# An mLSTM and mixture-of-experts attention kernel on one core: a rebuilt front, expert ranks on GpSimd and ScalarE, a shorter PSUM hold, and values loaded without zeros

## Chip, cores and metric

The kernel runs on one core of one Trainium2 chip. The metric is device time in microseconds of one execution. Before the change the median of three runs is 352.0 us (350.49 to 353.44).

## The reference

For 4 sequences of 768 tokens and 8 heads of 40, an mLSTM recurrence with exponential gates and a running maximum produces x (768 x 320 for each sequence). Four experts then run causal attention over x, and each token takes the weighted sum of its two best experts.

```python
m_new = np.maximum(f_gate[:, :, t] + m, i_gate[:, :, t])
f_stab = np.exp(f_gate[:, :, t] + m - m_new)
i_stab = np.exp(i_gate[:, :, t] - m_new)
C = f_stab * C + i_stab * outer(v_t, k_t)
n = f_stab * n + i_stab * k_t
y_t = sigmoid(o_gate_t) * (C @ q_t) / np.maximum(np.abs(n @ q_t), 1.0)
...
logits = x @ w_gate
topk = np.argpartition(-logits, K, axis=-1)[..., :K]
w = softmax over the two logits that were taken
for e in range(E):
    q, k, v = x @ wq[e], x @ wk[e], x @ wv[e]
    a = causal softmax of scale * (q @ k.T)
    out += (w of the tokens that took e) * (a @ v @ wo[e])
```

## The kernel before

**How it is written.** Nothing is issued directly. `Tape.add` records every operation, and `Tape.plan` (L339 on) simulates the five engines and the DMA queue with a cost for each operation (`cost`), and writes down the order in which it placed them. `emit` (L541) then issues them in that order, so L541 is the line of nearly every instruction. Within an engine the order is fixed. Between engines semaphores hold. A change of one operation or of one cost therefore re-orders the whole program.

**Part 1** is the mLSTM in 24 chunks of 128 tokens (4 sequences, 6 chunks each), each cut into two sub-chunks of 64. `gates` works out the running maximum m, the gates' sums G and the input factor for 32 rows (sequence and head) in three segments of tokens: 0 to 127, 128 to 383, 384 to 767. `gates_out` transposes the input factor and writes it to `cN`; `decays` makes the factors `dec` of the carried state. `p1_prep` makes the decay matrix `dm` and the weighted keys `ks`; `p1_intra` makes scores within the chunk; `p1_inc` steps the state (`cd`, `sts`); `p1_scale` multiplies the queries `kqs` by exp(G); `p1_state` adds the part within the chunk (matmuls of `nat` and `dm`) and the carried part (matmuls of `kqs` and `sts`) in one PSUM bank, divides, and multiplies by the output gate into `xt`; `p1_out` transposes to `xh` and `xl`, a high and a low half.

For the first three chunks (the front) `dm` and the factor on `kqs` come from TensorE matmuls that spread G over the partitions. For all others they come from DRAM: G and exp(G) are written to `gd` and `ge` and read back, spread over partitions, as `dm` and `eqs`.

**Part 2** is the attention in 8 units (a sequence's half, 384 tokens). Its head is three `values`, two `queries`, two `keys` and `gate`, which makes the logits' ranks `rk` and the weights `ew`. Then come scores (`big` banks), softmax (`A`), transposes (`AT`), `mix` (with the shares `facb`, made from `ew`) and `project` to `ob` and the output. Units overlap with later chunks of part 1; the two are interleaved by hand in `flow`.

**Buffers and queues.** PSUM has four banks `one` and two pairs `big`. Nearly all DMAs go through SyncE's queue, in order. Each chunk brings 2 for `kqs`, 2 for `qbd`, 2 for `dm`, 2 for `eqs` and 1 for `nat`. The `nat` tile holds a chunk's keys (320 columns), its values in 656 columns, of which half are zeros (so that a sub-chunk's matmul sees its own 64 tokens only), and its output gate (320).

**Dummies.** 16 matmuls of zeros (`wz`) open the program. 60 more are spares: `choose` puts one where the next group of matmuls is more than 200 ns away, before it looks for another group that could start.

Of the kernel before, what the change touches and what calls it, by code (L numbers as in the profile page):

```python
# [33 lines left out]
    ("nat", 3, NNAT),  # L34
# [30 lines left out]
C_IDENT, C_CAUS, C_HALF, C_INDB = 0, 128, 192, 194  # L65
C_SEL = C_INDB + 4
C_MASK = C_SEL + 4 * GR
NKV = DM + 2 * H * D1


def const_table():
# [13 lines left out]
    t[64:, C_HALF] = 1.0  # L85
    t[:, C_HALF + 1] = 1.0
    t[64:, C_HALF + 1] = -1.0
# [73 lines left out]
class Tape:  # L161
# [95 lines left out]

    def cut(self):
        self.open = None


    def cost(self, op):
        n = max([x.free_size() for x in op.ins + op.outs[:1]] or [1])
        psum = any("PSUM" in str(x.space) for x in op.ins)
        if op.call == "dma_start":
# [16 lines left out]
            return 600.0, total / d * (10 + d * 0.05) / k, k, 1600.0  # L282
        if op.eng == "tensor":
            return (0.0, 0.0)
        if op.call == "memset":
            return (n / 1.2 + 60, 40) if op.eng == "gpsimd" else (n * 0.52 + 8, 75)
        if op.eng == "gpsimd":
            inner = any([s for s, c in x.ap if c > 1][-1:] == [0] for x in op.ins)
            return (120 + n * (1.85 if inner else 2.32), 40) if op.call != "tensor_copy" else (130 + n * 2.0, 40)
        if op.eng == "scalar":  # L290
            return n / 1.2 + (53 if psum else 93) + (95 if len(op.outs) > 1 else 0), 120
        if op.call == "tensor_tensor_scan":
            return n * 2.1 + 120, 92
        if op.call == "tensor_tensor_reduce":
            return n * 1.0417 + 230, 92
# [12 lines left out]
    def plan(self):  # L308
# [47 lines left out]
        free = dict.fromkeys(ENGINES, 700.0)  # L356
        colfree, mode, order = [700.0] * 4, None, []
        rings = [0.0] * 16
        pool = [0.0, 0.0]
# [54 lines left out]
        def choose():  # L414
# [7 lines left out]
            if spares:  # L422
                b = self.home(spares[0])
                if b.ring.holder[b.slot or 0] is b:
                    x = begin(spares[:1])
                    if x is not None and (s is None or s - x > STALL):
                        return x, 0, spares[:1]
# [19 lines left out]
            if best:  # L447
                return best
            return (s, 0, todo[0]) if s is not None else None

        while len(order) < len(ops) + spare:
            best = None
            for e in ENGINES:
                if e == "tensor":
                    c = choose()
                else:
                    cand = []
                    for op in avail[e]:
# [4 lines left out]
                        if op.call == "dma_start":  # L463
                            s = max(s, op.late + shift - HOLD)
# [48 lines left out]
            if op.call == "dma_start":  # L513
# [5 lines left out]
                op.end = en + 700  # L519
            else:  # L520
                if e == "vector" and pool[0] < s < pool[1] and blocked(op):
                    s = pool[1]
                free[e] = s + op.cost[0]
# [35 lines left out]
def mlstm_moe_kernel(ctx, tc, kq, nat, ig, fg, wqkv, wo, const, out):  # L559
# [63 lines left out]
    eqs = [keep(f"eqs{i}", [GR, 4, P], F32) for i in range(2)]  # L623
    sts = [keep(f"sts{i}", [GR, 4, 2, D1], F32) for i in range(6)]
    qls = [keep(f"qls{i}", [P, 2, HALF], F32R) for i in range(3)]
    gd = dram("gd", [B * H, S])
    ge = dram("ge", [B * H, S])
    cN = keep("cN", [P, NCH, 2, B, 4], F32)
    gend = gtail.rearrange("p (b j) -> p b j", b=B)
# [33 lines left out]
    def load_nat(b, j, t=None, part=None):  # L663
        if t is None:
            t = buf("nat", [P, NNAT], F32)
        cs = slice(0, NNAT) if part is None else (slice(0, NKV), slice(NKV, NNAT))[part]
        (nc.sync.dma_start(t[:, cs], nat[b, j][:, cs]))
        return t

# [23 lines left out]
    def gates(c0, c1, eng):  # L693
# [5 lines left out]
        nc.gpsimd.tensor_tensor(i_sb[:, cs], i_sb[:, cs], m_sb[:, cs], op=ALU.subtract)  # L699
        yield  # L700
        eng.tensor_tensor(f_sb[:, n0:c1], f_sb[:, n0:c1], m_sb[:, n0 - 1 : c1 - 1], op=ALU.add)
        eng.tensor_tensor(g_sb[:, n0:c1], f_sb[:, n0:c1], m_sb[:, n0:c1], op=ALU.subtract)
        eng.tensor_scalar(g_sb[:, cs], g_sb[:, cs], -104.0, None, op0=ALU.max)
        yield
        nc.vector.tensor_tensor_scan(G_sb[:, cs], rmask[:, cs], g_sb[:, cs], 0.0, op0=ALU.mult, op1=ALU.add)
        gdone.append(nc.gpsimd.tensor_tensor(i_sb[:, cs], i_sb[:, cs], G_sb[:, cs], op=ALU.subtract))
# [912 lines left out]
```

## Time and profile before

| | us |
|---|---|
| median of 3 runs (lowest, highest) | 352.0 (350.49, 353.44) |
| profiled execution, its own time | 352.23 |
| its span, first to last instruction | 350.5 |
| PE / PEld busy | 324.0 (92%) / 275.1 (79%) |
| DVE busy | 265.8 (76%) |
| ACT busy | 217.7 (62%) |
| POOL busy | 188.7 (54%) |

PE is TensorE's matmuls, PEld its weight loads, DVE is VectorE, ACT is ScalarE, POOL is GpSimd, and SPq is SyncE's queue, which issues DMAs. Busy PE counts each matmul's latency, not its share of the array, so 92% is not 92% of peak. Tiles are named without their numbers. A group's row gives its count, total busy us, mean ns, and the idle time ahead of it.

### The profile page before, as it was taken

Reading aid. Unit: us, or ns where it says so; the run is one execution under the profiler, and the core shown is the slowest. Engines: PE = TensorE matmul, PEld = TensorE weight load, DVE = VectorE, ACT = ScalarE, POOL = GpSimd, SP = SyncE. Lnnn points to the kernel's source line nnn. Section 1 sums busy time; section 2 is a strip of 40 time slices with the busy share of each in tenths; the row PEclk is TensorE's granted clock in tenths of the full one; section 3 lists DMA queues with packets and bytes.
Section 4 is the critical chain, followed back from the end, with each engine's and each line's share of the span. In section 5 each row is a group of like instructions: output and inputs, shape, how many; then the busy total and the mean of one; then the engine's idle time right before and its main releaser. Section 6 shows DMA issues by size and latency. Waiting matters only on the chain.

```text
span 350.5 us, 9216 instructions
## 1 busy us (share of the span) xinstructions
PE 324.0 (92%) x3312; PEld 275.1 (79%) x3312; DVE 265.8 (76%) x787; ACT 217.7 (62%) x591; POOL 188.7 (54%) x267
## 2 busy tenths in 40 slices
PE   8789998899998998899999998799999999999994
PEld 3576696798887887588998787679998887988882
DVE  7999389879888867669888767569888766677673
ACT  5673245776785776544785666534785776567752
POOL 4783698689758456648538456638547221241000
PEclk9999999999999999999999999999999999999999
DMA  7999929957375266427585257427570100101001
GB/s 200 288 240 230 214 76 242 240 146 199 117 194 140 49 186 191 109 80 186 163 196 154 38 143 220 112 51 212 173 197 6 56 0 2 39 20 38 21 21 37
DMA packets 40653, 45.78 MB, mean 131 GB/s; under 512 B 3808, under 2 KB 34752, under 8 KB 40608
## 3 DMA queue, kind: packets, MB, share of 16 engines
q1 hardware_dynamic: 40560, 45.10, 49.1%
q8 instruction: 26, 0.43, 0.5%
q14 instruction: 19, 0.16, 0.2%
q10 hardware_dynamic: 48, 0.10, 0.1%
HBM read 41.06 MB, written 4.13 MB: 129 GB/s over the span
## 4 chain that ended last, share of the span: by engine, by line
PE 56%; DVE 23%; issue 6%; ACT 6%; DMA 5%; POOL 2%; SPq 1%; DVEq 0%; POOLq 0%; ACTq 0%
PE one L541 48%; PE big L541 8%; DVE AT L541 4%; DVE sts L541 3%; DMA dm<-gd 2%; DVE KS L541 2%; DVE one L541 2%; DVE A L541 2%; DMA eqs<-ge 2%; ACT A L541 2%; ACT AT L541 2%; DVE rk L541 2%; DVE den L541 1%; DVE xt L541 1%; ACT KS L541 1%
## 5 line engine op out<-in xcount | busy, mean ns | idle before, releaser
L541 ACT ACTIVATE A<-A,nmx 128x128 f32<-128x128 f32 (+5 forms) x96 | 63.7, 666 | 18.1 <-DVE nmx L541 17.7
L541 DVE CUSTOM_DVE_ANT_0 A<-big,maskw 128x128 f32<-128x128 f32 (+5 forms) x96 | 58.1, 618 | 6.1 <-PE big L541 4.5
L541 PE MATMUL one<-cst,A 128*128 128x128 f32 x336 | 53.1, 277 | 8.4 <-ACT AT L541 3.1
L541 PEld LDWEIGHTS one<-cst,A 128*128 128x128 f32 x336 | 39.5, 140 | 16.6 <-ACT AT L541 4.6
L541 ACT ACTIVATE AT<-one 128x512 f32<-128x512 f32 (+2 forms) x101 | 41.0, 427 | 17.4 <-PE one L541 11.2
L541 PE MATMUL big<-KS,QD 128*128 128x384 f32 (+4 forms) x128 | 44.6, 357 | 1.0 <-DVE nmx L541 0.8
L541 PE MATMUL one<-AT,V 128*64 128x384 f32 (+2 forms) x360 | 40.1, 368 | 0.4 <-DVE R L541 0.4
L541 PE MATMUL big<-KS,qls 128*128 128x384 f32 (+4 forms) x128 | 40.2, 322 | 0.0
L541 POOL TENSOR_TENSOR cd<-sts,dec 112x328 f32<-112x328 f32 x37 | 27.4, 742 | 20.2 <-DVE sts L541 19.6
L541 POOL TENSOR_TENSOR dm<-dm,cst 128x512 f32<-128x512 f32 x21 | 27.0, 1287 | 20.0 <-DMA dm<-gd 14.2
L541 PEld LDWEIGHTS one<-AT,V 128*64 128x64 f32 x360 | 22.8, 137 | 15.8 <-issue 12.3
L541 PE MATMUL one<-xh,WH 128*128 128x384 f32 x96 | 34.4, 358 | 0.2
L541 PE MATMUL one<-xl,WH 128*128 128x384 f32 x96 | 32.4, 337 | 0.0
L541 POOL TENSOR_TENSOR kqs<-kqs,eqs 112x512 f32<-112x512 f32 x21 | 26.9, 1283 | 6.5 <-DMA eqs<-ge 6.2
L541 DVE TENSOR_TENSOR sts<-one,cd 40x164 f32<-40x164 f32 x80 | 25.7, 321 | 5.0 <-POOL cd L541 3.0
L541 PEld LDWEIGHTS big<-KS,QD 128*128 128x128 f32 x128 | 24.4, 191 | 2.3 <-DVE nmx L541 1.4
L541 DVE SCALAR_TENSOR_TENSOR qls<-one,QD 64x384 fp32r<-64x384 f32 x32 | 17.7, 554 | 11.2 <-ACT QD L541 7.1
L541 PE MATMUL one<-qbd,kqs 112*64 112x128 f32 x384 | 26.2, 278 | 0.0
L541 DVE COPY AT<-one 128x128 f32<-128x128 f32 (+2 forms) x55 | 19.1, 370 | 7.2 <-PE one L541 4.3
L541 POOL TENSOR_TENSOR yl<-R,yh 128x384 fp32r<-128x384 f32 x14 | 14.2, 1011 | 19.3 <-ACT yh L541 13.3
L541 PEld LDWEIGHTS big<-KS,qls 128*128 128x128 f32 x128 | 24.3, 190 | 0.0
L541 POOL TENSOR_TENSOR dm<-dm,cN 128x512 f32<-128x512 f32 x21 | 22.3, 1063 | 3.1 <-DVE cN L541 2.0
(122 smaller groups left out, 813.6 us busy)
## 6 DMA issues: line engine op xcount, KB each, us to landing
nat<-in_nat SPq DMA_DIRECT2D x21, 648.0 KB, 5.8
kqs<-in_kq SPq DMA_DIRECT2D x48, 192.0 KB, 5.9
dm<-gd SPq DMA_DIRECT2D x42, 128.0 KB, 3.2
qbd<-in_kq SPq DMA_DIRECT2D x42, 96.0 KB, 3.1
eqs<-ge SPq DMA_DIRECT2D x42, 96.0 KB, 5.5
out<-ob SPq DMA_DIRECT2D x24, 160.0 KB, 4.2
nat<-in_nat SPq DMA_DIRECT2D x3, 488.0 KB, 7.0
A<-in_wqkv SPq DMA_DIRECT2D x2, 386.0 KB, 8.3
```

Of the source, the lines that this page charges most:

```text
L541: f(*[fix(x) for x in op.a], **{k: fix(v) for k, v in op.k.items()})
```

## The change

**Values without zeros.** `nat` becomes three fixed tiles `nats`, whose zero blocks are written once by GpSimd. A chunk's values, keys and output gate arrive in three DMAs (upper 64 rows, lower 64 rows, output gate), 324 KB for values and keys in place of 488 KB. `vals` gives matmuls the same 82 columns as before, as a strided view.

**Gates on VectorE.** In the first two segments the two subtractions that make the input factor go from GpSimd to VectorE, and come after the second scan; in the third segment the planner picks either engine (`tape.either`). `gates_out` uses small matmuls that place the sub-chunks where `cN` needs them, so one VectorE copy takes the place of four. For the first three chunks it also transposes G, and ScalarE writes `eG` = exp(G) with a row for each token.

**Carried part scaled behind the matmul.** For the first three chunks `p1_scale` is gone: its eight spreading matmuls and the multiplication of `kqs` by their result. In `p1_state` the carried part goes to a PSUM bank of its own (`pi`); VectorE multiplies it by `eG` into `pc` and adds `pc` to `py`. `pb` of `p1_prep` moves from a `one` bank to a `big` one.

**Expert ranks.** Seven comparisons on VectorE give way to a subtraction (GpSimd), Sign (ScalarE), an added table (GpSimd), Sign (ScalarE), the sum as before (VectorE), Sign (ScalarE), and two 12-element operations (GpSimd) in place of one on VectorE.

**Shorter PSUM hold.** In `p1_state` the magnitude goes to SBUF tiles `two`, and the product with the output gate goes straight to SBUF, so `py` is read for the last time there; the last multiplication reads SBUF and may go to either engine.

**Set-up.** The correction of the third weight block becomes a plain high and low split; the low halves are cut into nine pieces for either engine. Six VectorE memsets of `AT` become two, one of `qbd` goes to ScalarE, two of `sts` go from GpSimd to ScalarE.

**Planner.** New cost figures, an opening table load on ScalarE, at most eight DMAs in flight, and GpSimd's hold on VectorE counted when candidates are ranked. Spares come after the look for another group.

```diff
-            return 600.0, total / d * (10 + d * 0.05) / k, k, 1600.0
+            return 480.0, total / d * (12 + d * 0.055) / k, k, 1600.0
...
-            if spares:
-                b = self.home(spares[0])
...
             best = None
...
             if best:
                 return best
+            if spares:
+                b = self.home(spares[0])
...
                         if op.call == "dma_start":
-                            s = max(s, op.late + shift - HOLD)
+                            s = max(s, op.late + shift - HOLD, landed[e][-8] if len(landed[e]) > 7 else 0.0)
...
+        if part != 1:
+            nc.sync.dma_start(t[0:T, 0 : NV + DM], nat[b, j, 0:T, 0 : NV + DM])
+            nc.sync.dma_start(t[T:P, NV : NV + DM + NV], nat[b, j, T:P, 0 : NV + DM])
+        if part != 0:
+            nc.sync.dma_start(t[:, NKV:], nat[b, j][:, NV + DM :])
...
-        nc.gpsimd.tensor_tensor(i_sb[:, cs], i_sb[:, cs], m_sb[:, cs], op=ALU.subtract)
...
+        eng(i_sb[:, cs], i_sb[:, cs], m_sb[:, cs], op=ALU.subtract)
+        gdone.append(eng(i_sb[:, cs], i_sb[:, cs], G_sb[:, cs], op=ALU.subtract))
...
-        for a in range(2):
-            for sub in range(2):
-                nc.vector.tensor_copy(
...
+        nc.vector.tensor_copy(
+            cN[:, ja:jb].rearrange("p j s b c -> p (j s b c)"), pg[:, ja * 32 : jb * 32]
+        )
...
+            nc.scalar.activation(eG[:, ja * H : jn * H], pg[:, 256 + ja * H : 256 + jn * H], AF.Exp)
...
-        hi = buf("A", [P, NW], F32R)
-        nc.scalar.activation(hi, raws[2], AF.Copy, scale=cst[:, C_HALF + 1 : C_HALF + 2])
-        nc.vector.scalar_tensor_tensor(
-            WH[:, 2, :], raws[2], cst[:, C_HALF : C_HALF + 1], hi.bitcast(F32), op0=ALU.mult, op1=ALU.add
-        )
+        for c in (slice(NQK, NW), slice(0, 2 * P), slice(2 * P, NQK)):
+            for kt in range(2):
+                tape.either(WL[:, kt, c], raws[kt][:, c], WH[:, kt, c], op=ALU.subtract)
+            tape.either(WH[T:, 2, c], raws[2][T:, c], WH[T:, 2, c].bitcast(F32), op=ALU.subtract)
...
-            nc.vector.tensor_tensor(qc, pe[:GR].rearrange("r (g t) -> r g t", g=4), qc, op=ALU.mult)
...
+            nc.vector.tensor_tensor(
+                pc[r].rearrange("p (h d) -> p h d", d=D1),
+                pi[r, : H * D1].rearrange("p (h d) -> p h d", d=D1),
+                eG[r, j * H : (j + 1) * H, None].to_broadcast([n, H, D1]),
+                op=ALU.mult,
+            )
+            nc.vector.tensor_tensor(py[r, : H * D1], py[r, : H * D1], pc[r], op=ALU.add)
...
-        nc.vector.tensor_scalar(den, nm2, 2.0, None, op0=ALU.max)
-        nc.vector.reciprocal(den, den)
-        nc.vector.scalar_tensor_tensor(pyv[:, :, 0:D], eo, 1.0, pyv[:, :, 0:D], op0=ALU.add, op1=ALU.mult)
-        nc.vector.tensor_tensor(eo, pyv[:, :, 0:D], den[:, :, None].to_broadcast([P, H, D]), op=ALU.mult)
+        nc.vector.tensor_reduce(den, twos, axis=AX.X, op=ALU.max)
+        nc.vector.scalar_tensor_tensor(eo, eo, 1.0, pyv[:, :, 0:D], op0=ALU.add, op1=ALU.mult)
+        nc.vector.reciprocal(den, den)
+        tape.either(eo, eo, den[:, :, None].to_broadcast([P, H, D]), op=ALU.mult)
...
-            for e in range(E):
-                if e > 0:
-                    nc.vector.tensor_tensor(
-                        rk[:, :, e, 0:e], lg[:, :, 0:e], lg[:, :, e : e + 1].to_broadcast([P, 3, e]), op=ALU.is_ge
-                    )
-                nc.vector.tensor_tensor(
-                    rk[:, :, e, e:E], lg[:, :, e:E], lg[:, :, e : e + 1].to_broadcast([P, 3, E - e]), op=ALU.is_gt
-                )
...
+            g.tensor_tensor(
+                rk,
+                lg[:, :, None, :].to_broadcast(full4),
+                lg[:, :, :, None].to_broadcast(full4),
+                op=ALU.subtract,
+            )
+            nc.scalar.activation(rf, rf, AF.Sign)
+            g.tensor_tensor(rk, rk, ahead[:, None].to_broadcast(full4), op=ALU.add)
+            nc.scalar.activation(rf, rf, AF.Sign)
             nc.vector.tensor_reduce(rank, rk, axis=AX.X, op=ALU.add)
-            nc.vector.scalar_tensor_tensor(ew, rank, 1.5, ew, op0=ALU.is_lt, op1=ALU.mult)
+            nc.scalar.activation(rr, rr, AF.Sign, bias=1.0)
+            g.tensor_tensor(rank, rank, ew, op=ALU.mult)
+            g.tensor_tensor(ew, ew, rank, op=ALU.subtract)
```

## Rows read from the trace of the kernel before

**Rows 1.** The windows view: busy time of each engine in four stretches (the front, the stretch after it, the long middle, the end), then granted clock, DMA share and GB/s.

```profile
0.00:43.00 43.00, 36.98 (x409) 25.36 (x411) 35.01 (x81) 23.07 (x64) 25.91 (x40) 1.00 0.97 236
43.00:71.00 28.00, 25.27 (x303) 22.65 (x300) 23.35 (x76) 16.05 (x50) 22.79 (x31) 1.00 0.80 188
71.00:312.00 241.00, 229.00 (x2320) 199.33 (x2319) 183.10 (x558) 155.36 (x420) 137.15 (x194) 1.00 0.45 122
312.00:351.00 39.00, 32.80 (x290) 27.81 (x288) 24.39 (x73) 23.23 (x59) 2.85 (x4) 0.97 0.08 26
```

**Rows 2.** The chain of work that ended last, its shares by line, in the stretches 0 to 43, 43 to 71 and 71 to 351 us.

```profile
by line: DVE AT L541 27.7%; PE one L541 14.0%; issue 12.5%; PE big L541 7.3%; DVE sts L541 7.1%; DVE WH L541 5.0%; DVE kqs L541 3.7%; DVE dm L541 3.2%; DVE cN L541 3.1%; DVE one L541 3.1%; DVE xt L541 2.3%; DVE den L541 2.2%; DVE qbd L541 2
...
by line: PE one L541 34.0%; DMA dm<-gd 16.5%; DMA nat<-in_nat 14.0%; DVE sts L541 4.1%; SPq L541 4.0%; issue 3.8%; DVE A L541 3.7%; ACT A L541 3.4%; DVE dm L541 2.4%; ACT AT L541 2.4%; DVE KS L541 2.0%; PE big L541 1.9%; DVE xt L541 1.8%; D
...
by line: PE one L541 55.0%; PE big L541 8.2%; issue 5.6%; DVE sts L541 2.4%; DVE KS L541 2.2%; DMA eqs<-ge 2.1%; DVE rk L541 2.0%; ACT AT L541 1.8%; DVE A L541 1.7%; ACT A L541 1.7%; DVE one L541 1.5%; ACT KS L541 1.4%; DMA dm<-gd 1.2%; DVE
```

**Rows 3.** Pieces of the same chain in order of time: start us, length us, what.

```profile
7.55 3.21 DVE AT L541 x8
...
30.77 2.15 DVE WH L541
...
39.59 3.13 PE big L541 x14
...
51.40 3.93 DMA nat<-in_nat
...
57.47 4.61 DMA dm<-gd
```

**Rows 4.** VectorE's groups by form, all but one of which stand in the front: count, busy us, mean ns, idle time ahead.

```profile
L541 DVE MEMSET AT<- 32x384 f32 x6 | 2.3, 378 | 0.7
...
L541 DVE MEMSET qbd<- 112x1024 f32 x1 | 0.9, 912 | 0.2 <-issue 0.2
...
L541 DVE COPY cN<-one 64x48 f32<-64x48 f32 x4 | 0.8, 205 | 0.2 <-PE one L541 0.2
L541 DVE COPY cN<-one 64x32 f32<-64x32 f32 x4 | 0.8, 188 | 0.1
...
L541 DVE COPY cN<-one 64x16 f32<-64x16 f32 x4 | 0.7, 164 | 0.1
...
L541 DVE TENSOR_TENSOR kqs<-one,kqs 112x512 f32<-112x512 f32 x3 | 2.1, 687 | 0.1
...
L541 DVE SCALAR_TENSOR_TENSOR WH<-A,cst,A 128x772 fp32r<-128x772 f32 x1 | 2.2, 2155 | 0.0
...
L541 DVE TENSOR_TENSOR WL<-A,WH 128x772 fp32r<-128x772 f32 x1 | 1.0, 952 | 0.0
...
L541 DVE TENSOR_TENSOR cd<-sts,dec 112x328 f32<-112x328 f32 x3 | 2.4, 809 | 0.1
...
L541 DVE TENSOR_TENSOR AT<-AT,AT 32x256 f32<-32x256 f32 x2 | 1.4, 683 | 0.0
...
L541 DVE SCALAR_TENSOR_TENSOR one<-xt,one 128x320 f32<-128x320 f32 x24 | 11.8, 493 | 7.9 <-ACT one L541 7.7
```

**Rows 5.** GpSimd's groups by form, for prices.

```profile
L541 POOL TENSOR_TENSOR WL<-A,WH 128x772 fp32r<-128x772 f32 x1 | 1.8, 1845 | 0.0
...
L541 POOL TENSOR_TENSOR ks<-nat,dm 128x320 f32<-128x320 f32 x24 | 18.0, 748 | 6.7 <-ACT dm L541 2.2 <-PE one L541 2.0 <-DMA nat<-in_nat 1.2
...
L541 POOL TENSOR_TENSOR ew<-lg,mx 128x12 f32<-128x12 f32 x8 | 1.7, 217 | 5.8 <-DVE mx L541 5.8
```

**Rows 6.** DMA issues: count, KB each, median us from issue to landing.

```profile
nat<-in_nat SPq DMA_DIRECT2D x21, 648.0 KB, 5.8
...
nat<-in_nat SPq DMA_DIRECT2D x3, 488.0 KB, 7.0
```

**Rows 7.** The ranks: VectorE's groups by form, one of ScalarE's small groups, and ScalarE's table load.

```profile
L541 DVE TENSOR_TENSOR rk<-lg 128x9 f32<-128x9 f32 x16 | 5.4, 367 | 0.0
...
L541 DVE TENSOR_TENSOR rk<-lg 128x6 f32<-128x6 f32 x16 | 4.3, 296 | 0.0
...
L541 DVE TENSOR_TENSOR rk<-lg 128x3 f32<-128x3 f32 x16 | 4.0, 278 | 0.0
...
L541 DVE SCALAR_TENSOR_TENSOR ew<-rank,ew 128x12 f32<-128x12 f32 x8 | 2.9, 360 | 0.5
...
L541 DVE TENSOR_TENSOR rk<-lg 128x12 f32<-128x12 f32 x8 | 2.6, 321 | 0.0
...
L541 ACT ACTIVATE ew<-ew 128x12 f32<-128x12 f32 x8 | 1.6, 205 | 0.0
...
L541 ACT ACT_TABLE_LOAD x1 | 1.3, 1283 | 1.2 <-PEq L1606 1.2
```

**Rows 8.** GpSimd's timeline between 92 and 107 us: the weights `ew` of one unit are ready, and the first use of them in `facb`.

```profile
98.30 0.22 POOL L541 TENSOR_TENSOR ew<-ew,ws 128x12 f32<-128x12 f32 x1 [0.47 <-DVE ws L541]
...
105.85 0.83 POOL L541 TENSOR_TENSOR facb<-fac,ew 128x384 f32<-128x384 f32 x1
```

**Rows 9.** Who waited for whom, over the span (TensorE's row: from 43 us on): total us, times, longest us.

```profile
PE one L541 <- DVE xt L541: 2.4, 5, 1.4
...
POOL ew L541 <- DVE mx L541: 5.8, 2, 5.0
...
SPq L541 <- PE one L541: 116.6, 46, 9.8
```

More of the change, by code (lines that the diff above doesn't have):

```diff
@@ L68 @@
 NKV = DM + 2 * H * D1
+NV = H * D1
 def const_table():
@@ L356, in plan @@
         free = dict.fromkeys(ENGINES, 700.0)
+        table = 1280.0
         colfree, mode, order = [700.0] * 4, None, []
         rings = [0.0] * 16
+        landed = {e: [] for e in ENGINES}
         pool = [0.0, 0.0]
@@ L448, in choose @@
                 return best
+            if spares:
+                b = self.home(spares[0])
+                if b.ring.holder[b.slot or 0] is b:
+                    x = begin(spares[:1])
+                    if x is not None and (s is None or s - x > STALL):
+                        return x, 0, spares[:1]
             return (s, 0, todo[0]) if s is not None else None
@@ L519, in plan @@
                 op.end = en + 700
+                landed[e].append(op.end)
             else:
@@ L522, in plan @@
                     s = pool[1]
+                if e == "scalar":
+                    s, table = s + table, 0.0
                 free[e] = s + op.cost[0]
@@ L623, in mlstm_moe_kernel @@
     eqs = [keep(f"eqs{i}", [GR, 4, P], F32) for i in range(2)]
+    nats = [keep(f"nat{i}", [P, NNAT], F32) for i in range(3)]
     sts = [keep(f"sts{i}", [GR, 4, 2, D1], F32) for i in range(6)]
     qls = [keep(f"qls{i}", [P, 2, HALF], F32R) for i in range(3)]
+    two = [keep(f"two{i}", [P, H, 2], F32) for i in range(2)]
     gd = dram("gd", [B * H, S])
@@ L885, in p1_inc @@
                 cd = buf("cd", [GR, 4, 2, D1], F32)
-                (nc.vector if first(b, j) and sub else nc.gpsimd).tensor_tensor(
+                (tape.either if first(b, j) else nc.gpsimd.tensor_tensor)(
                     cd.rearrange("p g z d -> p g (z d)"),
@@ L903, in p1_scale @@
         if dm_from_pe(b, j):
-            pe = one(f"pe_{b}_{j}")
-            for g in range(4):
-                for z in range(2):
-                    nc.tensor.matmul(
-                        pe[z * T : z * T + T, g * P : (g + 1) * P],
-                        ident[:, z * 4 + g : z * 4 + g + 1].to_broadcast([P, T]),
-                        full[:, j * P : (j + 1) * P],
-                        start=g == 0,
-                        stop=g == 3,
-                    )
-            nc.vector.tensor_tensor(qc, pe[:GR].rearrange("r (g t) -> r g t", g=4), qc, op=ALU.mult)
             return
@@ L931, in p1_state @@
                     dm[:, c, sub, :],
-                    v1[:, sub, c, :],
+                    vals(nt, sub, c),
                     start=c == 0,
-                    stop=c == 3 and j == 0 and sub == 0,
+                    stop=c == 3 and (pi is not py or j == 0 and sub == 0),
                 )
@@ L946, in p1_state @@
                         sin[sub][:, 2 * g + a, :, :],
-                        start=False,
+                        start=pi is not py and g == 0 and a == 0,
                         stop=g == 1 and a == 1,
@@ L1575, in pairs, with halves @@
         return t.reshape(B, NCH, P, 8 * n)
-    def blocks(a):
-        n = a.shape[-1]
-        t = _np.zeros((B, NCH, 2, T, 2, 4, 2, n), a.dtype)
-        w = a.reshape(B, 4, 2, NCH, 2, T, n).transpose(0, 3, 2, 5, 4, 1, 6)
-        for i in range(2):
-            t[:, :, i, :, :, :, i] = w[:, :, i]
-        return t.reshape(B, NCH, P, 16 * n)
+    def halves(a, c):
+        return _np.concatenate(
+            [_np.concatenate(x, axis=-1) for x in ((a[:, :, :T], c[:, :, :T]), (c[:, :, T:], a[:, :, T:]))], axis=2
+        )
     def groups(a):
@@ L1595 @@
         "kq": _np.concatenate([groups(k), groups(q)], axis=-1),
-        "nat": _np.concatenate([pairs(k), blocks(v1), rows(o)], axis=-1),
+        "nat": _np.concatenate([halves(pairs(v1), pairs(k)), rows(o)], axis=-1),
         "ig": inputs["i_gate"],
```

152 lines of the change are left out of this document (85 added, 67 removed).

## The prediction

> **What bounds the kernel now.** I read the windows view first. In all four stretches the granted clock is 0.97 or 1.00, so TensorE runs at 2.4 GHz throughout [rows 1]. In the first 43 us two resources are close to full at once: VectorE is busy 35.0 of 43 us, and the DMA engines 0.97 of it, at 236 GB/s [rows 1]. From 43 to 71 us GpSimd (22.8 of 28) and the DMA engines (0.80) lead beside TensorE [rows 1]. From 71 to 312 us TensorE is busy 229 of 241 us; the DMA share drops to 0.45 and VectorE still holds 183 [rows 1]. The reader is to see three kernels in one: a front that VectorE and DMA share, a short stretch of loads, and a long middle that belongs to TensorE with VectorE some way behind.
>
> Then the chain of waits, stretch by stretch, because a busy share does not say which work came last. In the front the gate tiles on VectorE have 27.7% of it, and other VectorE tiles another 30% or so [rows 2]; its longest pieces are eight gate operations in a row (3.21 us), the correction of the third weight block (2.15) and 14 dummy matmuls (3.13) [rows 3]. From 43 to 71 us one load of `nat` (3.93) and one of `dm` (4.61) stand on it [rows 3]. From 71 us on TensorE has 63% of it, and VectorE's rank comparisons 2.0% [rows 2].
>
> **Part by part: the front's VectorE work.** What leaves it for certain: six memsets of `AT` at 0.378 (2.27 us), one of `qbd` (0.91), twelve copies into `cN` (2.3), three products on `kqs` (2.06) and the weight correction (2.16): 9.7 us [rows 4]. What comes: two memsets at 0.378 (0.76); three copies into `cN`, at about 0.21 each as the widest of the old (0.62); for three chunks a product and a sum over 328 columns, priced as the output-gate product of 320 columns, 6 x 0.493 (2.96); and two subtractions for each of two gate segments, 2 x 0.683 for 256 columns and half of that for 128 (2.05): 6.4 us [rows 4]. That is 3.3 us less. Between engines lie the low halves of the weights, three blocks of 772 columns at 0.952 on VectorE or 1.845 on GpSimd; three products `cd` at 0.809; and three last multiplications at 0.49, or 0.75 on GpSimd by `ks` [rows 4, 5]. With half of each on VectorE this is 1.43 + 1.21 + 0.73 against 0.95 + 2.43 + 1.46 before, 1.5 us less. The sum is 4.8 us less out of 35.0. The ends: all of it on VectorE gives 3.3 - 1.9 = 1.4 us less; all of it on GpSimd, which is idle 17 of 43 us, gives 3.3 + 4.84 = 8.1 us less [rows 1].
>
> **The front's DMA.** A chunk's values and keys shrink from 488 to 324 KB [rows 6]. Five chunks are asked for before 43 us, so 0.82 MB less, at 236 GB/s 3.5 us [rows 1, 6]. This is what a front filled by DMA can give, whatever VectorE does.
>
> **The dummies.** 14 dummies fill 3.13 us of the chain, in which the planner saw nothing close enough at the head of its list [rows 3]. After the change it looks for another group first. The least this gives is nothing (no free bank, or the work is not ready), the most 3.1 us. I take 1.0, a third: part 2's first projections are there to be pulled forward, but part 1's own matmuls, which follow next, still wait for their operands.
>
> **Front, summed.** The later of the two resources counts: 3.5 us by DMA against 4.8 by VectorE, so 3.5, and 1.0 from the dummies: 4.5 us, with ends at 1.4 and 9. ScalarE takes over the clearing of `qbd` (0.91 at VectorE's price) and two small exponentials at about 0.2; it is idle 20 of 43 us, which hides them; without that cover they would cost 1.3 us [rows 1, 4, 7]. The new bank `pi` gives the carried part's matmuls no wait for `kqs`, and I count nothing for it.
>
> **From 43 to 71 us.** The load of `nat` on the chain loses a quarter of its bytes: 648 KB become 484, so about 1.0 of 3.93 us [rows 3, 6]. The load of `dm` behind it waited on full engines; the same tenth off a chunk's bytes gives 0.5 of 4.61 [rows 3]. Sum 1.5 us; ends nothing (SyncE's two more issues a chunk use it up) and 2.6 (three chunks at 0.164 MB and 188 GB/s) [rows 1, 6].
>
> **The middle.** The ranks' seven comparisons cost VectorE 16.3 us in 8 units and the masking 2.9; on the chain they have 2.0% of 280 us, 5.6 us [rows 2, 7]. In their place come three operations on ScalarE at about 0.205 each and four on GpSimd, at 0.22 for 12 elements and about 0.28 for 48 (between the 12 and 320 columns' rows) [rows 5, 7]. About 2.4 us of VectorE goes for each unit, and some 1.6 us of two engines with more idle time comes. These lie beside other work as long as `ew` is early: in the unit shown it is ready 7.3 us before `facb` uses it [rows 8]. When an operation leaves the chain, the next one behind it comes on, so of the 5.6 us I count half, 2.8; the ends are nothing and all 5.6. The shorter PSUM hold frees a bank about 0.7 us earlier for each chunk (a reciprocal and a product), but TensorE waited for `xt` 2.4 us in all [rows 9]: counted at nothing, at most 2.4. SyncE issues 42 more DMAs in the later chunks; its queue stood 116.6 us waiting for TensorE to free tiles, and these hide the issues [rows 9].
>
> **The sum.** 4.5 + 1.5 + 2.8 = 8.8 us off the profiled execution's 352.2 us gives 343.4. That execution is 0.2 us above the median of the three runs, so the two can be taken as one.
>
> **Rivals.** *The loads hold the front.* Every later chunk needs `gd` and `ge` written, read back, and a tile freed; if these set the pace, an earlier front only waits longer at 51 and 57 us, where the chain already goes through two loads [rows 3]. Against it: they have fewer bytes to move, and tiles come free earlier. Then only the `nat` load and the ranks are left: 352.2 - 1.0 - 2.8 = 348.4.
>
> *More comes back.* If the planner fills all 3.1 us of dummies, VectorE loses its 4.8 and DMA does not hold it, and the ranks give their whole 5.6, the time is 352.2 - 7.9 - 1.5 - 5.6 = 337.2. For it: VectorE, not DMA, ends most of the front's waits [rows 2]. Against it: the DMA share of 0.97 [rows 1].
>
> *The ranks' hand-offs stall ScalarE (slower).* Each Sign stands in ScalarE's queue until GpSimd has finished, and the exponentials and the copies out of PSUM, for which TensorE waits, stand behind it. The order is fixed ahead, so any lateness of GpSimd becomes a stall. GpSimd's first small operation in this chain waited up to 5.0 us for VectorE [rows 9]. With 24 Signs, a wait of 2 us each and half of it on the path, 24 us are added and the ranks' 2.8 not won: 352.2 - 6.0 + 24 = 370. It decides from 6.0 / 12 = 0.5 us of mean wait, and is slower by over 1% from 0.8, which is 356. Against it: ScalarE is idle 86 of 241 us in the middle, and the planner places each Sign behind its source [rows 1].
>
> *Sign needs a table of its own.* The trace has one table load of 1.283 us, for exp, tanh, abs and copy together [rows 7]. If Sign is not in that table, each of 8 rankings loads at least twice, 16 x 1.283 = 20.5 us on ScalarE; half of it on the path gives 343.4 + 10.3 = 353.7. The Trainium skill ("ScalarE: Activation LUTs", Table sets: the hidden batching unit) says that a change of set is paid for each switch and that cheap functions such as relu, copy, identity and abs fill every set; it does not list Sign there. By the Trainium skill's figure of about 2.66 us a switch (same page, What ACT_TABLE_LOAD costs) the 16 would be an estimated 42.6 us. The trace agrees for abs and copy; no run here shows Sign. It is as plain a function as abs, so this is unlikely.
>
> *It doesn't do what it says.* The re-ordered program may lose elsewhere what the front wins; then 352.
>
> **How the numbers follow.** The forecast has 0.50, its own range is 339 to 347. Loads hold the front 0.17 (346 to 350), more comes back 0.15 (334 to 339), hand-offs 0.10 (354 and up), a table 0.03, nothing 0.05. The time is that of the likeliest, 343.4. The range from 335.5 to 351 leaves out the slower cases and the far end of the gains, which are the front's 9 us, all 5.6 of the ranks and 2.6 of the loads (335.0). About 1% is what a measurement of this kernel can tell from no change, 348.5 to 355.5. Faster by over 1%: 0.50, 0.15, and 0.10 of the loads' case, 0.75. Within: the rest of that case, nothing, and a little of the table, 0.13. Slower: 0.12.
>
> **What would show it.** Right: the matmuls that follow the 14 dummies start near 38 us in place of 42.7; fewer `wz`; VectorE busy about 30 us in the first 43; `rk` gone from the chain; one table load; `nat` issues of 162 KB; GpSimd and ScalarE each busier by 5 to 9 us over the span. Wrong: loads of `dm`, `eqs` or `nat` with over 9 us on the chain before 71 us; ScalarE's Signs with long idle time ahead put down to GpSimd; more than one table load; a middle that is as long as before (241 us) although VectorE is freer.

## The result and the profile after

| | before | after |
|---|---|---|
| median of 4 runs each, taken together on one chip, us | 352.72 (350.49 to 357.45) | 340.92 (338.95 to 343.28) |
| ratio, 95% interval | | 0.9689 [0.9597, 0.978] |
| profiled execution, its own time / span, us | 352.23 / 350.5 | 341.03 / 339.3 |
| DVE / ACT / POOL busy, us | 265.8 / 217.7 / 188.7 | 247.7 / 214.2 / 211.8 |

The medians differ by 11.8 us. The ratio leaves out the slow execution of the kernel before (357.45 us) and gives 11.0 us, where 8.8 was forecast. The windows view of the changed kernel, in the columns of [rows 1] (its last stretch ends at 340 us):

```profile
0.00:43.00 43.00, 38.94 (x453) 29.91 (x455) 33.36 (x83) 26.40 (x73) 30.72 (x46) 0.96 0.91 206
43.00:71.00 28.00, 25.76 (x322) 22.77 (x319) 22.08 (x74) 17.94 (x61) 27.02 (x41) 1.00 0.94 202
71.00:312.00 241.00, 231.00 (x2311) 202.79 (x2310) 175.26 (x513) 156.89 (x435) 154.09 (x238) 1.00 0.44 109
312.00:340.00 28.00, 22.94 (x217) 18.89 (x215) 16.99 (x52) 13.02 (x34) 0.00 (x0) 0.99 0.11 37
```

GpSimd has become nearly full from 43 to 71 us (27.0 of 28, [rows 1] 22.8), and carries 17 us more from 71 to 312 us, where VectorE has lost 8. The chain of waits of the changed kernel, by line, from 0 to 43, 43 to 71 and 71 to 340 us, as [rows 2]:

```profile
by line: PE one L555 32.4%; PE big L555 27.4%; DVE sts L555 8.8%; DVE cd L555 7.3%; POOL cd L555 3.1%; DVE dm L555 3.1%; issue 2.5%; DVE one L555 2.4%; DVE facb L555 2.3%; DVE xt L555 2.2%; POOL ks L555 1.7%; DVE ks L555 1.1%; DVE den L555 
...
by line: DMA nat<-in_nat 25.2%; PE one L555 10.6%; issue 9.7%; POOL kqs L555 9.0%; POOL QD L555 5.4%; POOL wol L555 5.4%; POOL cd L555 5.2%; POOL dm L555 3.7%; DVE xt L555 3.3%; POOL maskw L555 3.1%; POOL ws L555 2.9%; POOL qls L555 2.8%; P
...
by line: PE one L555 52.3%; PE big L555 8.7%; issue 5.5%; DMA eqs<-ge 4.5%; DVE A L555 3.1%; POOL kqs L555 2.9%; SPq L555 2.6%; DVE sts L555 2.1%; POOL cd L555 1.9%; DVE KS L555 1.7%; DMA qbd<-in_kq 1.4%; DVE AT L555 1.0%; ACT A L555 1.0%; 
```

The gates (`DVE AT`, 27.7% of the front) and VectorE's ranks (`DVE rk`, 2.0% of the rest) are gone from these rows. Of the ranks' new operations some stand on the chain: from 43 to 71 us two pieces of `POOL rk`, 0.22 and 0.25 us. TensorE has 60% of the front's chain, 7.02 us of it the opening dummies; in the second stretch GpSimd's small tiles stand between two loads of `nat` (3.62 and 3.44 us). Groups of the changed kernel, as [rows 4], [rows 5] and [rows 7]: count, busy us, mean ns, idle time ahead and its releaser:

```profile
L555 PE MATMUL big<-wz 128*128 128x512 bf16 x36 | 11.2, 444 | 1.0 <-DVE wz L555 1.0
...
L555 POOL TENSOR_TENSOR xt<-xt,den 128x320 f32<-128x320 f32 x17 | 12.6, 744 | 3.7 <-DVE den L555 3.5
...
L555 ACT ACTIVATE rk<-rk 128x48 f32<-128x48 f32 x16 | 3.8, 240 | 6.4 <-POOL rk L555 6.1
...
L555 POOL TENSOR_TENSOR rk<-lg 128x48 f32<-128x48 f32 x8 | 2.5, 311 | 5.2 <-DVE lg L555 5.2
L555 POOL TENSOR_TENSOR rk<-rk,cst 128x48 f32<-128x48 f32 x8 | 2.3, 288 | 1.0 <-ACT rk L555 0.7
...
L555 ACT ACTIVATE rank<-rank 128x12 f32<-128x12 f32 x8 | 1.6, 201 | 0.3 <-DVE rank L555 0.3
L555 ACT ACT_TABLE_LOAD x1 | 1.3, 1283 | 1.2 <-PEq L1645 1.2
```

There is one table load, as before, so Sign shares a table with the others. The 24 Signs had 6.4 + 0.3 us of idle time ahead of them, 0.28 each. Dummies (`wz`) are down to 36. Before, the same group had 55, the last of them started at 55.4 us:

```profile
L541 PE MATMUL big<-wz 128*128 128x512 bf16 x55 | 14.6, 414 | 1.0 <-DVE wz L541 1.0
...
L541 PE MATMUL big<-wz x55: 379/379/634, 1.0 to 55.4; 128*128 128x512 bf16 x55
```

To see where the time came from, I read starts of the same matmuls off both timelines. A unit's values begin with the first matmul into `one` with `WH` as its first operand and `xh` as its second; its queries' projection with the two exchanged. Before (start us, length us): the first unit's values, the first projection, the values of the second, the third and the eighth unit.

```profile
31.81 0.37 PE L541 MATMUL one<-WH,xh 128*128 128x260 f32 x1
...
43.35 0.44 PE L541 MATMUL one<-xh,WH 128*128 128x384 f32 x1
...
57.30 0.39 PE L541 MATMUL one<-WH,xh 128*128 128x260 f32 x1
...
85.29 0.28 PE L541 MATMUL one<-WH,xh 128*128 128x260 f32 x1
...
285.96 0.36 PE L541 MATMUL one<-WH,xh 128*128 128x260 f32 x1
```

The changed kernel: the same, without the second unit's values (51.1 us).

```profile
28.06 0.47 PE L555 MATMUL one<-WH,xh 128*128 128x260 f32 x1
...
36.19 0.52 PE L555 MATMUL one<-xh,WH 128*128 128x384 f32 x1
...
79.64 0.28 PE L555 MATMUL one<-WH,xh 128*128 128x260 f32 x1
...
276.12 0.37 PE L555 MATMUL one<-WH,xh 128*128 128x260 f32 x1
```

The lead is 3.8 us at the first values, 7.2 at the first projection, 5.7 at the third unit, 9.8 at the eighth and 11.2 at the end of the span. So not all of the 7.2 us lasts to 80 us, and about half of the whole is won after it.

### The profile page after: what moved, and what is told of

The parts are those of the page before. It is cut to its first block, busy times and chain, and to the rows that moved or that the text cites. A ratio compares the mean times of both kernels' runs of the same rounds, so it can differ in the third digit from the quotient of the medians.

```text
span 339.3 us, 9199 instructions
## 1 busy us (share of the span) xinstructions
PE 318.6 (94%) x3293; PEld 274.4 (81%) x3293; DVE 247.7 (73%) x719; ACT 214.2 (63%) x601; POOL 211.8 (62%) x323
## 4 chain that ended last, share of the span: by engine, by line
PE 57%; DVE 13%; POOL 11%; DMA 7%; issue 5%; ACT 3%; SPq 2%; POOLq 0%; DVEq 0%; ACTq 0%
PE one L555 46%; PE big L555 10%; DMA eqs<-ge 4%; POOL kqs L555 3%; DVE sts L555 3%; DVE A L555 2%; POOL cd L555 2%; SPq L555 2%; DMA nat<-in_nat 2%; DVE KS L555 1%; DMA qbd<-in_kq 1%; POOL ks L555 1%; POOL QD L555 1%; DVE xt L555 1%; DVE cd L555 1%
## 5 line engine op out<-in xcount | busy, mean ns | idle before, releaser
L555 PE MATMUL one<-cst,A 128*128 128x128 f32 x336 | 51.2, 276 | 5.1 <-ACT AT L555 1.8
L555 ACT ACTIVATE AT<-one 128x128 f32<-128x128 f32 (+2 forms) x97 | 37.9, 412 | 20.3 <-PE one L555 12.7
L555 POOL TENSOR_TENSOR cd<-sts,dec 112x328 f32<-112x328 f32 x38 | 28.7, 756 | 16.2 <-DVE sts L555 15.7
L555 PEld LDWEIGHTS one<-AT,V 128*64 128x64 f32 x360 | 22.8, 137 | 16.1 <-issue 12.0
L555 PE MATMUL one<-qbd,kqs 112*64 112x128 f32 x384 | 26.9, 284 | 2.9 <-DVE facb L555 2.5
L555 PEld LDWEIGHTS one<-qbd,kqs 112*64 112x64 f32 x384 | 21.1, 139 | 6.9 <-DVE facb L555 2.7
L555 DVE COPY AT<-one 128x128 f32<-128x128 f32 (+2 forms) x59 | 23.2, 406 | 4.2 <-PE one L555 3.5
```

The source lines that it names most:

```text
L555: f(*[fix(x) for x in op.a], **{k: fix(v) for k, v in op.k.items()})
```

## The experiments

The theory after the result: the time comes from the order of TensorE's work (the planner places real work before dummies) and from VectorE work taken out, in the front, in the ranks and in the last multiplications. The rivals: it comes from the smaller loads, or from the carried part scaled behind the matmul; and GpSimd's and VectorE's collisions give some of it back. A further rival weighs on each experiment: every edit re-orders the whole program, and order alone can move the time.

Each run has its ratio to the kernel before, measured in the same series on one chip. What a part is worth is worked out as the distance of that ratio from the changed kernel's, which was measured in two series (0.9689, and 0.9635 in the run again below), times 352.7 us: hence two numbers. The intervals are about 0.006 to 0.009 to either side, 2 to 3 us, and a distance has those of both its ends, so one under about 3 us is not told from nothing by the ratio alone. The four edits below that are read as no difference have ratios from 0.9601 to 0.9678, though each has an order of its own, with the third unit's values at 79.2 to 82.0 us.

A part of the scatter goes with TensorE's granted clock. The eight executions of the changed kernel took 338.95 to 340.56 us where the mean clock was 0.998 to 1.000 of 2.4 GHz (three), 340.81 and 341.03 at 0.995, and 343.28 to 343.92 at 0.989 or 0.990 (three).

**The planner alone.** The kernel before, with the new planner:

```
-            return 600.0, total / d * (10 + d * 0.05) / k, k, 1600.0
+            return 480.0, total / d * (12 + d * 0.055) / k, k, 1600.0
...
-            if spares:
-                b = self.home(spares[0])
...
             best = None
...
                 return best
+            if spares:
+                b = self.home(spares[0])
```

> The kernel before with nothing but the new planner (costs, at most eight DMAs in flight, GpSimd's hold when candidates are ranked, spares after the look for another group). If the changed operations made the gain, this gives the dummies' 1 us and little else: 349 to 352 us, the first queries' projection still at 42 to 43.5 us. If the new order made it, 342 to 346 us and that projection near 38.

Measured: 347.62 us, 0.9843 [0.9756, 0.9929]; 5.5 us off, between the two forecasts. Its timeline (first projection; values of the second and the eighth unit):

```profile
37.47 0.44 PE L554 MATMUL one<-xh,WH 128*128 128x384 f32 x1
...
55.18 0.39 PE L554 MATMUL one<-WH,xh 128*128 128x260 f32 x1
...
282.86 0.36 PE L554 MATMUL one<-WH,xh 128*128 128x260 f32 x1
```

The first projection comes 5.9 us earlier, but the second unit's values only 2.1 (57.3 before), the third's 1.8 (83.50), the eighth's 3.1, and the span ends 4.6 earlier (345.9). A matmul pulled into a dummy's place early is not the gain itself; the order keeps giving later too.

**The change without the planner.** The reverse: the changed kernel with the old costs and the old order.

> The changed kernel in the order of the old planner. If the changed operations made the gain: 341 to 344 us, first queries' projection at 36 to 38 us. If the new order made it: 346 to 350 us.

Measured: 345.57 us, 0.9767 [0.9689, 0.9844]; 2.8 to 4.7 us slower than the changed kernel, again between the forecasts. `wz` rises from 36 to 58 (15.9 us), and the first projection starts at 40.6 us (36.2 in the changed kernel). From the eighth unit's values to the end the old planner takes 64.5 us here and in the kernel before, the new one 63.0 with the planner alone and 63.2 in the changed kernel. Both directions agree: the planner is a large term, not 1 us.

**Dummies ahead of other work again.** The changed kernel with only that block put back, the costs new:

```
+            if spares:
+                b = self.home(spares[0])
...
             best = None
...
                 return best
-            if spares:
-                b = self.home(spares[0])
```

> The changed kernel whose planner puts a dummy before it looks for another group, as before; all else of the new planner stays. If this order is what the planner gave (run e2 lost 4.7 us without the new planner): 344 to 346 us, with the dummies after 11 us back from 12 to 25 or more. If the costs gave it: 340.5 to 342 us.

Measured: 344.64 us, 0.9709 [0.9654, 0.9764], against 0.9635 in the same series: 2.6 us slower, with 51 dummies and the first projection at 40.66 us. Its four executions (344.31 us and up) all lie above the twelve of the changed kernel and of the two other edits in that series (up to 343.92). By these numbers the few lines are worth about half or more of what the planner gives.

**The old ranks.** The changed kernel with the comparisons on VectorE:

```
-            nc.scalar.activation(rf, rf, AF.Sign)
...
+            for e in range(E):
+                if e > 0:
+                    nc.vector.tensor_tensor(
+                        rk[:, :, e, 0:e], lg[:, :, 0:e], lg[:, :, e : e + 1].to_broadcast([P, 3, e]), op=ALU.is_ge
+                    )
```

> The changed kernel with the seven comparisons and the masking back on VectorE. If the ranks were worth the 2.8 us that the prediction gave them: 343 to 345 us, with the first 70 us as in the changed kernel and the loss after that. If other work hides them: 340 to 341.5 us.

Measured: 345.34 us, 0.978 [0.9702, 0.9857]; 3.2 to 5.1 us slower. The third unit's values start at 81.8 us (79.6 in the changed kernel), the eighth's at 280.7 (276.1): 2.1 of it is lost by 80 us, 2.4 behind.

```profile
81.77 0.28 PE L555 MATMUL one<-WH,xh 128*128 128x260 f32 x1
...
280.69 0.37 PE L555 MATMUL one<-WH,xh 128*128 128x260 f32 x1
```

So the first 70 us were not as in the changed kernel, which the forecast for this run had assumed: the second unit's values already come at 52.9 us in place of 51.1.

**Planner and ranks together.** The kernel before with these two.

> The kernel before with two parts of the change alone: the new planner (run e1: 5.1 us) and the new ranks (run e3: some 4 us). If these two carry the gain and add up: 342.5 to 344.5 us. If the ranks are worth that much only behind the rebuilt front: 346 to 348 us.

Measured: 344.14 us, 0.9711 [0.9659, 0.9763]; 10.2 us off. All the rest of the change adds 0.8 to 2.7 us. The timeline says where (third and eighth unit's values):

```profile
80.63 0.28 PE L558 MATMUL one<-WH,xh 128*128 128x260 f32 x1
...
279.38 0.37 PE L558 MATMUL one<-WH,xh 128*128 128x260 f32 x1
```

With the old front and the old loads this run reaches the third unit 1.0 us after the changed kernel (0.4 by the second profile). From there to the eighth it takes 198.8 us, 2.3 more than the changed kernel (3.4 by the second profile): what the rest adds lies in the middle.

**The old PSUM hold and last multiplication.** The magnitude goes back to the bank too.

```
-        nc.vector.scalar_tensor_tensor(eo, eo, 1.0, pyv[:, :, 0:D], op0=ALU.add, op1=ALU.mult)
...
-        tape.either(eo, eo, den[:, :, None].to_broadcast([P, H, D]), op=ALU.mult)
...
+        nc.vector.scalar_tensor_tensor(pyv[:, :, 0:D], eo, 1.0, pyv[:, :, 0:D], op0=ALU.add, op1=ALU.mult)
+        nc.vector.tensor_tensor(eo, pyv[:, :, 0:D], den[:, :, None].to_broadcast([P, H, D]), op=ALU.mult)
```

> The changed kernel with the longer PSUM hold of before (magnitude, product and last multiplication through the bank, all on VectorE). The prediction counted the shorter hold at nothing, at most 2.4 us: 340.5 to 342.5 us. If the hold or the seventeen multiplications that went to GpSimd matter: 343.5 to 346 us.

Measured: 344.36 us, 0.9727 [0.9664, 0.979]; 1.3 to 3.2 us slower, at the edge of what the median tells. The timeline helps (third and eighth unit's values):

```profile
79.20 0.28 PE L555 MATMUL one<-WH,xh 128*128 128x260 f32 x1
...
278.42 0.37 PE L555 MATMUL one<-WH,xh 128*128 128x260 f32 x1
```

It reaches the third unit no later, and takes 199.2 us from there to the eighth; the changed kernel took 196.5 and, profiled again, 195.4. So the loss of about 3 us lies in the middle, as this edit would have it. TensorE waits again for VectorE's `xt`, 3.3 us in all over the span, as it did before the change:

```profile
PE one L541 <- DVE xt L541: 3.3, 6, 1.4
...
PE one L555 <- DVE xt L555: 3.3, 6, 2.0
```

The changed kernel's first profile lists no such wait, its second 1.3 us. But the run with the old ranks has 3.8 us of it with the hold as short as in the changed kernel, so the wait does not show the hold by itself. The run does not part the hold from the move of 17 of the 24 multiplications to GpSimd.

**The old front.** Gates, weight correction, clearing, `cd` and the scaling of `kqs` as before, all else new:

```
-        eng(f_sb[:, n0:c1], f_sb[:, n0:c1], m_sb[:, n0 - 1 : c1 - 1], op=ALU.add)
+        nc.vector.tensor_tensor(f_sb[:, n0:c1], f_sb[:, n0:c1], m_sb[:, n0 - 1 : c1 - 1], op=ALU.add)
...
+            nc.vector.tensor_tensor(qc, pe[:GR].rearrange("r (g t) -> r g t", g=4), qc, op=ALU.mult)
```

> The changed kernel with the whole front as before: gates partly on GpSimd, four copies into cN, products on kqs ahead of the matmul, weight correction and memsets on VectorE. If the front's VectorE time sets the end, as the prediction has it (3.3 to 4.8 us): 344.5 to 347 us, second unit's first values at 54 us or later. If the loads hold the stretch after the front: 341 to 343 us, with those values late but the middle's end not.

Measured: 344.49 us, 0.9703 [0.9647, 0.9758]; 0.5 to 2.4 us slower by the ratios, which is not told from nothing. The profiled execution, the slowest of its four (345.52 us), starts the second unit's values at 56.1 us and the third's at 83.5, 4.9 and 3.8 later than the changed kernel. Its timeline has TensorE waiting for `kqs` (idle time in brackets):

```profile
27.02 1.22 PE L558 MATMUL one<-sts,kqs 112*64 112x82 f32 x14 [2.89 <-DVE kqs L558]
```

Its windows from 26 to 32 us, the granted clock third from the end:

```profile
26.00:28.00 2.00, 0.98 (x14) 0.98 (x16) 1.92 (x5) 0.30 (x1) 0.32 (x1) 0.59 0.54 160
28.00:30.00 2.00, 2.00 (x23) 1.49 (x21) 1.94 (x5) 0.93 (x3) 0.77 (x2) 0.50 0.78 202
30.00:32.00 2.00, 2.00 (x26) 2.00 (x24) 0.76 (x3) 0.35 (x2) 1.48 (x2) 0.50 0.94 260
```

After that gap TensorE runs at 1.2 GHz for some 6 us. VectorE made `kqs` late because it spent 2.14 us ahead of it on a product that takes 0.71 in the changed kernel (mean of 7), beside a run of operations on GpSimd that ends at 24.77:

```profile
22.99 2.14 DVE L558 TENSOR_TENSOR xt<-xt,den 128x320 f32<-128x320 f32 x1
...
24.05 0.72 POOL L558 TENSOR_TENSOR ks<-nat,dm 128x320 f32<-128x320 f32 x1
```

That is the collision of the last section. What this profile shows is therefore a collision and the clock after it, and not the old front's own VectorE work alone; the run with planner and ranks, which has the old front too, reaches the third unit at 80.6 us. What the old front costs stays open.

**The old scaling alone.** Only the carried part goes back to `kqs` ahead of the matmul.

```
-        pi = one(f"pi_{nm}") if dm_from_pe(b, j) else py
+        pi = py
```

> The changed kernel with the carried part of the first three chunks scaled ahead of the matmul, as before. The prediction counted the new way as dearer for VectorE (2.96 us against 2.06) and nothing for the matmuls that wait no more. If only VectorE's time counts: 340 to 341.5 us. If the removed wait counts: 342.5 to 345 us, with the second unit's first values 1.5 us or more later than the changed kernel's 51.1 us.

Measured: 340.84 us, 0.9601 [0.9547, 0.9656], against 0.9635 in the same series: no difference.

**The zeros loaded again.** One DMA of 648 KB for a chunk instead of three.

```
-            nc.sync.dma_start(t[0:T, 0 : NV + DM], nat[b, j, 0:T, 0 : NV + DM])
-            nc.sync.dma_start(t[T:P, NV : NV + DM + NV], nat[b, j, T:P, 0 : NV + DM])
-            nc.sync.dma_start(t[:, NKV:], nat[b, j][:, NV + DM :])
+        nc.sync.dma_start(t[:, cs], nat[b, j][:, cs])
```

> The changed kernel with the zeros back in the load: one DMA of 648 KB a chunk in place of three of 484 KB (for the first three chunks 488 and 160 KB). If the front and the stretch after it are held by bytes, as the prediction has it (3.5 and 1.5 us): 344 to 346 us. If the two more issues a chunk use the bytes up: 340 to 342 us.

Measured: 342.52 us, 0.9657 [0.9591, 0.9724], against 0.9635: 0.8 us, no difference that the ratios can tell, and under what the loads were forecast to give. The third unit's values are 2.2 us late against the first profile of the changed kernel (81.8), the eighth's 0.6 (276.7). At equal clock there is some difference: this run's four executions had a mean clock of 0.997 to 0.999 and took 341.83 to 343.44 us, the changed kernel's two in the same series at 0.998 and 1.000 took 339.89 and 340.56. The run below that moves `cd` was as far off at 0.998 or more (342.01 to 342.58), so order alone could give that. The edit also takes away DMA issues, so it does not price bytes by themselves.

**Fewer bytes still.** No loads of `qbd` past the third chunk:

```
-        if not first(b, j):
-            for z in range(2):
-                nc.sync.dma_start(
-                    qb[z * 64 : z * 64 + RP, :, z, :],
...
```

> The changed kernel without the loads of the spread queries (qbd) past the third chunk, 192 KB and two issues less a chunk; the scores of those chunks use stale queries, so the output is not the reference's. If the loads hold the stretch from 43 to 71 us, as the rival of the prediction has it: the second unit's first values at 49 us and the third's at 77 in place of 51.1 and 79.6, 336.5 to 339 us in all. If they do not: 340 to 342 us.

Measured: 341.16 us, 0.9636 [0.9583, 0.9688]: no difference. Its windows view, second stretch:

```profile
43.00:71.00 28.00, 26.37 (x330) 22.10 (x329) 24.53 (x76) 18.36 (x61) 26.16 (x39) 1.00 0.57 148
```

The DMA share falls from 0.94 to 0.57 and the time stays; the second unit's values start at 53.5 us and the third's at 82.0, later than in the changed kernel and not earlier. A load of `nat` still stands on the chain there, behind TensorE's matmuls and SyncE's queue:

```profile
49.64 4.21 DMA nat<-in_nat
```

It took no less than the two in the changed kernel (3.62 and 3.44 us), though fewer bytes moved beside it.

**The front's `cd` on GpSimd only**, to take away a long VectorE operation (last section):

```
-                (tape.either if first(b, j) else nc.gpsimd.tensor_tensor)(
+                nc.gpsimd.tensor_tensor(
                     cd.rearrange("p g z d -> p g (z d)"),
```

> The changed kernel with the products cd of the first three chunks on GpSimd only. In the changed kernel one of them takes 2.78 us on VectorE at 18.35 us, TensorE then stands still for 2.48 us and its granted clock falls to 0.50 from 22 to 24 us. If that stall sets the front: first queries' projection at 33 to 34.5 us in place of 36.2, 337 to 339 us in all. If the loads hold the front: 340 to 341.5 us and the projection within 0.5 us of 36.2.

Measured: 342.25 us, 0.9678 [0.9608, 0.9747]: no difference that can be told. The clock stays at 1.00 from 18 to 26 us, but the collision only moves (last section), and the first projection starts at 39.3 us, which neither forecast had.

**The changed kernel again**, with another profile:

> The changed kernel once more, to stand beside the next runs: 340 to 342 us.

Measured: 342.13 us (339.89 to 343.92), 0.9635 [0.9558, 0.9711]. The median of its 8 executions in both series is 340.92. No version here beats it by more than its own scatter.

## Why the prediction was right, and where its sum was off

The direction and the chief parts were right: the front, the ranks and the planner's order each lie in the sum. By place, its first half held: the forecast had 4.5 + 1.5 = 6.0 us won by 71 us, and the lead at the third unit is 5.7 (5.1 in the second profile). The other half did not: 2.8 us were counted behind it, and 5.5 came. By cause, several terms were off even where the places fit, and that the total came near is partly luck: 5.0 of the 8.8 us were counted from the loads, for which no run shows that much, and the planner, priced at 1.0, and the hold, priced at nothing, made up for them.

- **The dummies, 1.0 us: too small.** The planner alone gave 5.5 us, without it 2.8 to 4.7 were lost, and the order of the dummies alone is 2.6. The step that failed was to price it from the one piece of 14 dummies in the chain [rows 3]. In the run with the planner alone the lead grows from 1.8 us at the third unit to 3.1 at the eighth and 4.6 at the end: the new order and costs gave 2.8 us behind 80 us, where no dummy ran any more. Which of them gave it (the costs, the limit of eight DMAs, GpSimd's hold on VectorE) no run parts.
- **The ranks, half of 5.6: the mechanism right, the size off.** Measured 3.2 to 5.1. Counting half because the next operation comes on was too careful: more than half of the share on the chain came back, by the second number nearly all.
- **The hold, 0: too small.** It and the last multiplications gave 1.3 to 3.2 us in the middle, about the upper end (2.4) that was written down from TensorE's waits for `xt` [rows 9].
- **The loads, 3.5 and 1.5 us: not there at that size.** The front was sized by DMA as the later of two resources from a share of 0.97 [rows 1], and the 0.5 us of `dm` by full engines. Zeros put back cost 0.8 us by the ratios and some 2 at equal clock, which order alone could give; 192 KB a chunk taken away gave nothing, and the run with planner and ranks, which loads the zeros, is 1.0 us late at the third unit. A high share said here that the engines had work under way, not that work waited for them.
- **VectorE in the front, 4.8 with ends at 1.4 and 8.1: not settled, likely small.** The old front costs 0.5 to 2.4 us by the ratios, and in the run with planner and ranks 1.0 by 80 us together with the loads; its own profile has more, with a collision in it. VectorE's busy time in the first 43 us fell to 33.4 (32.1 in the second profile), not to 30. Part of the difference is a product lengthened by 2.3 us (last section). The front's upper end of 9 us is no sum of the ends given for its parts (8.1 and 3.1).
- **The carried part behind the matmul, 0: right** when the rest is new. In the run with the old gates too, TensorE waited 2.89 us for `kqs`, behind a collision.

Taken away one at a time, planner, ranks, hold and front come to 2.8 + 3.2 + 1.3 + 0.5 = 7.8 us by their lower numbers and 4.7 + 5.1 + 3.2 + 2.4 = 15.4 by their upper; the whole is 11.0 to 12.9 by the two ratios. Planner and ranks together are shown from both sides: put in alone they gave 10.2, and each taken out costs 2.8 us or more. Whether the parts simply add is not to be told at this scatter.

Of the signs named ahead, these came: matmuls earlier (the first projection by 7.2 us), fewer `wz`, VectorE's `rk` off the chain (two short pieces of GpSimd's are on it), one table load, 162 KB issues. "GpSimd and ScalarE each busier by 5 to 9 us" did not: GpSimd gained 23.1 us, 12.6 by the last multiplications, and ScalarE lost 3.5. Loads of `nat` have 25.2% of 28 us, 7.1, on the chain from 43 to 71 us, under the 9 us named as a sign against the forecast; in the second profile `nat` (17.9%) and `dm` (13.2%) have 8.7 together. But that sign was badly chosen, since without `qbd` a load of `nat` stood on the chain too and the time was the same.

The rivals: *the loads hold the front* (346 to 350 us) falls with 340.9 and with the two runs on bytes. *Hand-offs* falls with the Signs' 0.28 us of mean idle time, below the 0.5 from which it decides. *A table for Sign* falls with one load of 1.283 us; the page of the Trainium skill named there ("ScalarE: Activation LUTs", Table sets) does not list Sign among the functions that fill every set, and the trace decides. *More comes back* (337.2) came in part: 340.9 lies between it and the forecast, through the planner and the ranks, not through its VectorE term.

What stays open: how much of the middle's gain is the shorter hold and how much the multiplications' move; what the rebuilt front and the smaller loads give; and what in the planner, beside the place of the dummies, gives time behind 80 us.

## What to carry to other kernels

When TensorE's order is planned ahead, look first at what its fillers push aside: letting ready work go before dummies cost a few lines and gave 2.6 us, no less than the rebuilt front is shown to give. A DMA share near 1 is no bound until a run with fewer bytes is faster. An engine's small operations on the chain can be worth more than half of their share there, if they are given to engines that have time where they wait. And where any edit re-orders the program, runs that should change nothing are needed to say what order alone does, and executions are best compared at the same granted clock.

## What the runs showed of the hardware that was not expected

A VectorE operation took six times its length beside GpSimd. VectorE's timeline of the changed kernel shows the same `cd` product twice:

```profile
18.35 2.78 DVE L555 TENSOR_TENSOR cd<-sts,dec 112x328 f32<-112x328 f32 x1
...
29.20 0.45 DVE L555 TENSOR_TENSOR cd<-sts,dec 112x328 f32<-112x328 f32 x1
```

GpSimd meanwhile, and TensorE behind it:

```profile
18.20 1.00 POOL L555 TENSOR_TENSOR AT<-AT,AT 32x384 f32<-32x384 f32 x1
19.17 0.23 POOL L555 TENSOR_TENSOR AT<-AT,cst 32x24 f32<-32x24 f32 x1
19.37 1.40 POOL L555 TENSOR_TENSOR WL<-A,WH 128x260 fp32r<-128x260 f32 x2
...
21.72 1.85 PE L555 MATMUL one<-qbd,kqs 112*64 112x128 f32 x16 [2.48 <-DVE facb L555]
```

VectorE's product ends at 21.13, when GpSimd's run of four operations, which ends at 20.77, and the product's own 0.45 are over: by these times it waited out the run, not one operation. The Trainium skill ("SBUF — State Buffer", Who interferes with whom) says that a VectorE instruction with both inputs in SBUF contends with a GpSimd instruction that reads SBUF; the rows agree, and they show how long it can last. TensorE stood idle 2.48 us for it, and ran at half clock behind, as the windows view of the changed kernel from 20 us shows:

```profile
20.00:22.00 2.00, 0.28 (x4) 0.28 (x6) 1.94 (x3) 0.05 (x1) 0.77 (x2) 0.97 0.62 168
22.00:24.00 2.00, 2.00 (x26) 2.00 (x24) 1.91 (x5) 1.03 (x6) 0.00 (x0) 0.50 1.03 259
```

In the second profile of the same program `cd` took 1.23 us: it ended at 19.77, 0.37 us after the first of GpSimd's operations, so it got in behind that one, and GpSimd's next took 0.48 us in place of 0.23. The first projection came 1.4 us earlier, and the clock stayed at 1.00. Rows of its timeline, then its windows from 20 us:

```profile
18.54 1.23 DVE L555 TENSOR_TENSOR cd<-sts,dec 112x328 f32<-112x328 f32 x1
...
18.41 0.99 POOL L555 TENSOR_TENSOR AT<-AT,AT 32x384 f32<-32x384 f32 x1
...
20.00:22.00 2.00, 1.65 (x32) 1.50 (x32) 1.91 (x4) 1.98 (x8) 1.05 (x2) 1.00 0.79 221
22.00:24.00 2.00, 0.74 (x18) 0.63 (x16) 1.91 (x8) 2.00 (x8) 1.72 (x3) 1.00 0.58 139
```

Of those 1.4 us nothing was left at the third unit (80.2 against 79.6). With `cd` moved to GpSimd, the collision falls on other products of VectorE, as its timeline shows:

```profile
20.41 1.29 DVE L555 TENSOR_TENSOR WL<-A,WH 128x260 fp32r<-128x260 f32 x1
...
23.14 2.25 DVE L555 TENSOR_TENSOR ks<-nat,dm 128x320 f32<-128x320 f32 x1
```

The same `ks` product took 0.48 us in the changed kernel. So the contention is not cured by moving one operation, and in the front it costs no time that a median shows. No profile was kept of an execution of the changed kernel at a mean clock of 0.989 or 0.990, so whether such collisions are what makes those some 3 us longer is not shown.
